# How batch 0 is fetched and normalised in the opening of a fused linear-attention and ELU-MLP kernel

## The chip, the cores and the metric

The kernel runs on one core of a Trainium2 chip. The metric is device time in microseconds (us) from launch to end. The kernel before took 285.53 us, the median of four runs that lie between 285.08 and 285.66 us. A separate execution was recorded by the hardware profiler; where the text speaks of the profile or the trace, it is that one execution.

## The reference, cut to what matters

```
kv  = einsum('bhsd,bhse->bhde', k, v)          # 8 batches, 8 heads, 576 positions, head size 64
out = einsum('bhsd,bhde->bhse', q, kv)
rms = sqrt(mean(out*out, axis=-1) + 1e-06)
att = out / rms * g_norm                       # per head
x   = att.transpose(0, 2, 1, 3).reshape(4608, 512)
h   = x @ w_in                                 # 512 -> 2048
g   = where(h > 0, h, exp(min(h, 0)) - 1)
y   = g @ w_out                                # 2048 -> 512
```

There is no softmax: each head has a 64 by 64 product K'V, which is multiplied by Q, normalised over the 64 features and scaled by a gain. The rest is a two-layer MLP. All inputs and the output are fp32; the kernel multiplies in bf16.

## The kernel before, in words

The 4608 rows of the MLP are worked in nine tiles of 512 rows. For each tile the kernel forms the normalised attention rows, turned so that features lie on partitions (`xT`), multiplies them by `w_in` (`mm1`, eight pairs of 128 columns, line 382), applies ELU (`elu`, lines 343 to 373) and multiplies by `w_out` (`mm2`, line 403). TensorE (PE) runs its instructions in the order in which the program issues them; there is no scheduler, since the whole program is recorded under a manual schedule, and each engine keeps program order.

Q, K and V of one batch are four chunks of 128 partitions by 576 numbers each; a chunk holds two heads. In fp32 a chunk is 288 KB, in bf16 144 KB. Tile 0 is mostly batch 0, and it is built chunk by chunk in a special opening (lines 577 to 652), which the change rewrites. For chunk c the steps are: `chunk_kv` (18 small matmuls, line 156), `chunk_kv_out` (VectorE (DVE) copies the product to SBUF, line 112), `chunk_y` (two matmuls of the turned Q with it, line 189), `chunk_square` (ScalarE (ACT), line 551), `mean_mm` (a matmul with a matrix of ones, line 199), a logarithm and an exponential on ACT for the inverse root (`inv_t` or `chunk_norm`), and `chunk_scale` (DVE, line 212), which writes row block c of `xT`. `early` (line 569) issues the first-layer matmuls of tile 0 for one row block c of `w_in` and `xT` at a time: pairs of columns (0,0) to (2,1), in the order c = 0, 2, 1, 3. `idle` (line 525) issues matmuls of zeros, as filling between waits.

Data comes on three issue queues. SyncE's queue (SP) brings chunks 0 and 2 of Q, and chunk 0 of K and of V, in fp32 into staging tiles, and `first_cast` turns them to bf16 on ACT and DVE. ACT's queue brings only the gain. GpSimd's queue (POOL) brings everything else and casts it to bf16 during the transfer: the other chunks of batch 0 (lines 488 to 494), then `w_in` in row blocks 0, 2, 1, 3 for the first six column blocks (line 496), the rest of `w_in`, then `w_out` alternating with batch 1, then batch 2. POOL's transfers take turns over eight semaphores, so the ninth is issued only when the first has landed, the tenth when the second has, and so on. Q is turned on PE with `ident` (`turned_q`, 16 transposes for two chunks, line 174) and copied out by DVE (`q_t_out`).

From batch 2 on Q arrives in fp32, is cast on POOL (`cast_q`, line 103), turned by a DMA transpose on SP's queue (`turn_q`, line 331), and only after that turn has landed does `after_turn` (line 339) let POOL issue the loads of the next batch. Attention rows of tiles from 2 on are also turned by DMA (`xT<-xs`, line 306) and then scaled by the gain (line 312).

## Time and profile before

| what | us |
|---|---|
| median of four runs | 285.53 |
| profiled execution, whole | 287.11 |
| its span, first to last instruction | 285.3 |
| PE busy in the span | 277.0 (97%) |
| DVE busy | 165.3 (58%) |
| ACT busy | 141.5 (50%) |
| POOL busy | 48.4 (17%) |
| granted TensorE clock | 0.999 of full |

The profile page gives busy time by engine, the span in 40 slices, the chain of work that ended last, and groups of like instructions. The timeline gives single groups of instructions in order of time: start, duration, engine, line, operation, and in brackets the idle time of the engine before it and what ended it. PE is matmul, PEld is the load of the stationary operand, which runs beside it. Matmuls are pipelined and their ends are modelled. The time from the issue of a transfer to its landing comes from the semaphore that tells of it.

### The profile page before, as it was taken

How to read it: one execution, taken by the hardware profiler on the slowest of the kernel's cores; microseconds unless marked ns; L12 is line 12 of the kernel's file. 1: busy time of each engine (PE TensorE's matmuls, PEld its weight loads, DVE VectorE, ACT ScalarE, POOL GpSimd, SP SyncE). 2: the span in 40 equal slices, each digit the busy share in tenths (PEclk: the TensorE clock that was granted, in tenths of full speed). 3: DMA queues.
4: the chain of work that ended last, by engine and by line, in shares of the span. 5: the costliest groups of instructions: out<-in, count | busy, mean ns of one | idle time of the engine just before them, and what ended most of it. 6: DMA issues, size and time to landing. Idle time of an engine off the chain costs nothing.

```text
span 285.3 us, 5154 instructions
## 1 busy us (share of the span) xinstructions
PE 277.0 (97%) x2123; PEld 128.9 (45%) x2123; DVE 165.3 (58%) x222; ACT 141.5 (50%) x209; POOL 48.4 (17%) x89
## 2 busy tenths in 40 slices
PE   7899999999799999999999999999999999999994
PEld 3434444443444444444444444444444444444443
DVE  3449532866487657854775378627763776344600
ACT  3778359694467355425552455345543554333311
POOL 7743303304340033032102220000000000000000
PEclk9999999999999999999999999999999999999999
DMA  7999999899996689779637971612150234020222
GB/s 210 191 204 206 207 263 224 199 283 128 183 292 83 142 168 251 99 181 256 159 36 159 261 166 40 150 45 74 39 110 0 74 39 110 0 76 0 74 74 75
DMA packets 50571, 39.46 MB, mean 138 GB/s; under 512 B 30964, under 2 KB 44020, under 8 KB 50548
## 3 DMA queue, kind: packets, MB, share of 16 engines
q0 software_dynamic: 15008, 21.30, 37.3%
q1 hardware_dynamic: 35136, 17.31, 29.3%
q10 hardware_dynamic: 404, 0.53, 0.5%
q8 instruction: 16, 0.26, 0.4%
q14 instruction: 7, 0.06, 0.1%
HBM read 36.70 MB, written 9.44 MB: 162 GB/s over the span
## 4 chain that ended last, share of the span: by engine, by line
PE 87%; DMA 6%; DVE 2%; ACT 2%; POOL 1%; issue 0%; SPq 0%; DVEq 0%; POOLq 0%
PE h_ps L382 40%; PE o_ps L403 39%; DMA xT<-xs 3%; DMA v_bf<-in_v_dram 2%; PE at L250 2%; PE at L156 1%; PE o_ps L440 1%; PE h_ps L569 1%; ACT elu_e L350 1%; DVE gT L366 1%; POOL k_bf L90 1%; PE mean L199 0%; PE qt_ps L174 0%; PE kv_ps L156 0%; PE y_ps L189 0%
## 5 line engine op out<-in xcount | busy, mean ns | idle before, releaser
L403 PE MATMUL o_ps<-w_out_sb,gT 128*128 128x512 bf16 x560 | 129.9, 379 | 0.0
L382 PE MATMUL h_ps<-xT,w_in_sb 128*128 128x512 bf16 (+1 forms) x560 | 128.0, 376 | 1.9 <-DVE xT L312 1.8
L350 ACT ACTIVATE elu_e<-h_ps 128x1024 bf16<-128x1024 f32 (+1 forms) x79 | 74.0, 953 | 91.3 <-PE h_ps L382 89.6
L403 PEld LDWEIGHTS <-gT 128*128 128x128 bf16 x560 | 54.3, 98 | 66.1 <-issue 0.9
L382 PEld LDWEIGHTS <-w_in_sb 128*128 128x128 bf16 x560 | 53.1, 98 | 63.3 <-issue 2.5
L366 DVE TENSOR_TENSOR gT<-elu_e,h_ps 128x1024 bf16<-128x1024 bf16 (+1 forms) x67 | 77.2, 1157 | 6.9 <-PE h_ps L382 0.5
L362 DVE TENSOR_SCALAR elu_e<-elu_e 128x1024 bf16<-128x1024 bf16 x72 | 31.9, 443 | 64.6 <-ACT elu_e L350 64.5
L419 ACT COPY o_sb<-o_ps 128x512 f32<-128x512 f32 x32 | 18.4, 588 | 21.2 <-PE o_ps L403 21.2
L103 POOL CAST q_bf<-st_q 128x384 bf16<-128x384 f32 x36 | 17.1, 519 | 42.1 <-DMA st_q<-in_q_dram 42.1
L283 DVE TENSOR_REDUCE ss<-sq 128x16 f32<-128x1024 bf16 x14 | 17.1, 1219 | 6.8 <-ACT sq L277 6.8
L299 DVE TENSOR_TENSOR xs<-at,ss 128x1024 bf16<-128x1024 f32 x14 | 17.1, 1219 | 1.9 <-ACT ss L292 1.9
L277 ACT ACTIVATE sq<-at 128x1024 bf16<-128x1024 f32 x14 | 14.4, 1028 | 0.0
L212 DVE SCALAR_TENSOR_TENSOR xT<-y_ps,g_col,rT 128x512 bf16<-128x512 f32 (+1 forms) x10 | 6.2, 640 | 10.1 <-ACT rT L209 8.0
L339 POOL COPY gate<-qT 1x16 bf16<-1x16 bf16 x5 | 1.1, 211 | 58.0 <-DMA qT<-q_bf 58.0
L355 ACT ACTIVATE elu_h<-h_ps 128x1024 bf16<-128x1024 f32 (+1 forms) x12 | 9.3, 821 | 0.0
L312 DVE TENSOR_SCALAR xT<-xT,g_col 128x1024 bf16<-128x1024 bf16 x14 | 6.7, 481 | 3.9 <-DMA xT<-xs 3.9
L156 PEld LDWEIGHTS <-k_bf 64*64 64x64 bf16 x576 | 6.4, 107 | 5.4 <-issue 5.4
L90 POOL DMA_DIRECT2D v_bf<-in_v_dram x11 | 7.8, 711 | 4.2 <-DMA w_in_sb<-in_moe_w_in_dram 2.1
L90 POOL DMA_DIRECT2D k_bf<-in_k_dram x11 | 7.7, 702 | 2.9 <-DMA w_in_sb<-in_moe_w_in_dram 2.2
L250 PEld LDWEIGHTS <-qT 64*128 64x128 bf16 (+1 forms) x248 | 4.3, 97 | 6.1 <-issue 5.9
L112 DVE COPY o_sb<-o_ps 128x256 f32<-128x256 f32 x1 | 0.4, 425 | 11.1 <-PE o_ps L440 11.1
L366 DVE TENSOR_TENSOR gT<-elu_e,elu_h 128x1024 bf16<-128x1024 bf16 x9 | 6.3, 704 | 0.8
(57 smaller groups left out, 101.4 us busy)
## 6 DMA issues: line engine op xcount, KB each, us to landing
st_q<-in_q_dram POOLq DMA_DIRECT2D x6, 1152.0 KB, 8.1
out_dram<-o_sb SPq DMA_DIRECT2D x24, 256.0 KB, 3.4
k_bf<-in_k_dram POOLq DMA_DIRECT2D x6, 576.0 KB, 10.4
v_bf<-in_v_dram POOLq DMA_DIRECT2D x6, 576.0 KB, 12.9
out_dram<-o_sb SPq DMA_DIRECT2D x19, 128.0 KB, 2.4
w_out_sb<-in_moe_w_out_dram POOLq DMA_DIRECT2D x4, 512.0 KB, 14.7
w_in_sb<-in_moe_w_in_dram POOLq DMA_DIRECT2D x2, 512.0 KB, 11.1
q_bf<-in_q_dram POOLq DMA_DIRECT2D x3, 288.0 KB, 13.4
```

The source lines that it names most:

```text
L90: eng.dma_start(out=dst.rearrange("p m j d -> p m (j d)"), in_=in_[:, ms, :])
L103: nc.gpsimd.tensor_copy(out=bf["q", b][:, u, js], in_=raw[b][:, u::2, js, :].rearrange("p l j d -> p j l d"),)
L250: nc.tensor.matmul(se_ps[lo:hi, l, (4 * i + m) * 64 : (4 * i + m) * 64 + 64], lhsT=qT[b][l * 64 : l * 64 + 64, s, u, j : j + n, :], rhs=kv ...
L277: nc.scalar.activation(sq, st["se", h], AF.Square)
L283: nc.vector.reduce_sum(out=ss, in_=st.pop(("sq", h)).rearrange("p l (m e) -> p (l m) e", e=D), axis=AX.X,)
L299: nc.vector.tensor_tensor(out=st["xs"][:, 2 * h : 2 * h + 2, :].rearrange("p i (l m e) -> p l i m e", l=2, e=D), in0=se_ps.rearrange("p l ...
L350: nc.scalar.activation(e[:, lo:hi, :], h, AF.Exp)
L362: nc.vector.tensor_scalar(out=e, in0=e, scalar1=1.0, scalar2=1.0, op0=ALU.min, op1=ALU.subtract)
L366: nc.vector.tensor_tensor(out=gT[T][:, 2 * i + lo : 2 * i + hi, :], in0=e[:, lo:hi, :], in1=h, op=ALU.add if relu else ALU.max,)
L382: nc.tensor.matmul((ps[a] if isinstance(ps, list) else ps[:, a, :])[:, cols], lhsT=w_in_sb[:, c, f * P : f * P + P], rhs=xT[T][:, c, cols] ...
L403: nc.tensor.matmul(o_ps[T, j], lhsT=gT[T][:, f, j * P : j * P + P], rhs=w_out_sb[:, f, :], start=(f == 0), stop=(f == FC - 1),)
L419: nc.scalar.copy(o_sb[T, half][:, j % 2, :], o_ps[T, j])
```

## The change: what it does

Six things are changed, all in the opening.

- On SP's queue now come chunk 0 of Q, then chunk 0 of V, then the gain; on ACT's queue comes chunk 0 of K. SP no longer brings chunk 2 of Q.
- Chunk 2 of Q is loaded on POOL's queue with a cast, ahead of everything else on that queue; it makes POOL's list of transfers one longer.
- The casts of chunk 0 are whole: Q on DVE, K and then V on ACT. DVE no longer casts a part of V, and ACT no longer casts a part of Q.
- Q of chunk 0 and of chunk 2 are turned apart, eight transposes and one 64-partition copy each (`turned_chunk`), instead of sixteen transposes and one 128-partition copy. Chunk 2 is turned after K'V of chunk 0.
- The product of chunk 0 with Q comes ahead of K'V of chunk 2. The logarithm of the first norm is issued before the square of chunk 2, and its exponential after it. The same is done with chunks 1 and 3: product and square of chunk 1 come ahead of K'V of chunk 3, and the mean and logarithm of chunk 1 ahead of the product and square of chunk 3 and of the first `early` group.
- The matmuls of zeros are 16 instead of 18, and the transpose of the gain comes after the first turn.

```diff
-    def first_load(name, cs):
+    def first_load(name, eng):
-        st = stage.tile([P, len(cs), RK, D], FP32, name=f"first_{name}", tag=f"first_{name}")
-        load(st, name, 0, slice(cs[0], cs[-1] + 1, 2), nc.sync)
+        st = stage.tile([P, 1, RK, D], FP32, name=f"first_{name}", tag=f"first_{name}")
+        load(st, name, 0, slice(0, 1), eng)
...
-    first = {"q": first_load("q", (0, 2)), "k": first_load("k", (0,)), "v": first_load("v", (0,))}
+    first = {}
+    for name, eng in (("q", nc.sync), ("k", nc.scalar), ("v", nc.sync)):
+        first[name] = first_load(name, eng)
...
-    nc.scalar.dma_start(out=g_row, in_=g_src)
+    nc.sync.dma_start(out=g_row, in_=g_src)
...
+    chunk_load("q", (2,))
     chunk_load("k", (2,))
     chunk_load("v", (2,))
...
+    def first_cast(name, eng):
+        copy_on(eng, bf[name, 0][:, 0:1], first[name])
+
+    def turned_chunk(l):
+
+        half = slice(l * 64, l * 64 + 64)
+        ps = as_bf16(single("m", "qt_ps"))
+        for j in range(8):
+            nc.tensor.transpose(ps[half, j * P : j * P + P], bf["q", 0][:, 2 * l, j, :], ident)
+        nc.vector.tensor_copy(
+            out=qT[0][half, :, 0, 0:8, :],
+            in_=ps[half].rearrange("p (j s r) -> p s j r", s=2, r=64),
+        )
...
-    idle(10, kv_ps[:, 0, :])
+    idle(9, kv_ps[:, 0, :])
+    first_cast("q", V)
+    first_cast("k", A)
+    turned_chunk(0)
     nc.tensor.transpose(g_ps[:, 0, 0:1], g_row.rearrange("o l e -> o (l e)"), one)
-    first_cast("q", (0, 2), V, low)
-    first_cast("q", (0, 2), A, high)
     nc.vector.tensor_copy(out=g_col, in_=g_ps[:, 0, 0:1])
-    ps = turned_q(0, 0, "m")
-    idle(3, kv_ps[:, 0, :])
-    first_cast("k", (0,), A, slice(0, RK))
-    q_t_out(0, 0, V, ps, slice(0, 8))
-    first_cast("v", (0,), A, high)
-    first_cast("v", (0,), V, low)
     mean = pair("A", "mean")[:, 0, :]
+    idle(2, kv_ps[:, 0, :])
+    first_cast("v", A)
     chunk_kv(kv_ps, 0)
     chunk_kv_out(kv_ps, 0, V)
+    turned_chunk(1)
+    chunk_y(0, single("x", "y_ps"))
+    chunk_square(0)
     chunk_kv(kv_ps, 2)
     chunk_kv_out(kv_ps, 2, V)
-    chunk_y(0, single("x", "y_ps"))
-    chunk_square(0)
-    idle(1, mean)
-    chunk_y(2, single("x", "y_ps"))
-    chunk_square(2)
     idle(1, mean)
     mean_mm(sq0[0], mean)
     r = r_tile()
-    inv_t(r[:, 0, :], mean)
-    mean = single("m", "mean")
+    nc.scalar.activation(r[:, 0, :], mean, AF.Ln, bias=eps_col)
+    chunk_y(2, single("x", "y_ps"))
+    chunk_square(2)
+    nc.scalar.activation(r[:, 0, :], r[:, 0, :], AF.Exp, scale=-0.5)
     ps = turned_q(0, 1, "m")
     q_t_out(0, 1, V, ps, slice(0, 8))
+    kv_ps = pair("B", "kv_ps")
+    h_ps = [pair("A", "h_ps")]
+    idle(1, h_ps[0][:, 0, :])
+    mean = single("m", "mean")
     mean_mm(sq0[2], mean)
     inv_t(r[:, 1, :], mean)
-    kv_ps = pair("B", "kv_ps")
-    h_ps = [pair("A", "h_ps")]
     chunk_kv(kv_ps, 1)
     chunk_kv_out(kv_ps, 1, V)
+    chunk_scale(0, r[:, 0, :])
     idle(2, h_ps[0][:, 0, :])
-    chunk_scale(0, r[:, 0, :])
+    chunk_y(1, single("m", "y_ps"))
+    chunk_square(1)
     chunk_kv(kv_ps, 3)
     chunk_kv_out(kv_ps, 3, V)
-    chunk_y(1, single("m", "y_ps"))
-    chunk_square(1)
     idle(1, h_ps[0][:, 0, :])
+    mean = single("m", "mean")
+    mean_mm(sq0[1], mean)
+    chunk_scale(2, r[:, 1, :])
+    r = r_tile()
+    nc.scalar.activation(r[:, 0, :], mean, AF.Ln, bias=eps_col)
     y3 = single("x", "y_ps")
     h_ps += [None, [single("x", "h_ps"), None]]
     chunk_y(3, y3)
     chunk_square(3)
-    chunk_scale(2, r[:, 1, :])
     h_ps[1] = pair("B", "h_ps")
     early([(0, 0), (0, 1)], 0)
-    mean = single("m", "mean")
-    mean_mm(sq0[1], mean)
-    r = r_tile()
-    nc.scalar.activation(r[:, 0, :], mean, AF.Ln, bias=eps_col)
     early([(1, 0), (1, 1), (2, 0)], 0)
```

## The prediction

> **What bounds the kernel now.** I read the page's busy shares, PE's waits, then the chain in order of time, then the timeline around each place where PE and a landing meet. The waits of PE come first:

> ```profile
> PE h_ps L382 <- DVE xT L312: 1.8, 1, 1.8
> PE kv_ps L525 <- DVE one L518: 1.2, 1, 1.2
> PE kv_ps L156 <- DVE v_bf L112: 0.5, 1, 0.5
> PE kv_ps L156 <- DVE kv_sb L112: 0.4, 1, 0.4
> PE kv_ps L156 <- DMA v_bf<-in_v_dram: 0.3, 1, 0.3
> PE h_ps L569 <- DVE xT L212: 0.2, 1, 0.2
> ```

> These 4.4 us are all of PE's larger waits: five before 16.4 us, one (1.8) at 71 us. A gain needs PE's useful work to slide forward, so I ask what holds it in place. The chain, in order of time (start, us, what):

> ```profile
> 4.95 7.02 DMA v_bf<-in_v_dram
> 11.97 0.14 issue
> 12.10 0.38 PE kv_ps L156 x13
> ...
> 14.22 0.70 ACT rT L632
> ...
> 16.32 2.17 PE h_ps L569 x9
> ...
> 62.56 9.64 DMA xT<-xs
> ```

> The opening's chain runs through V of chunk 3, which lands at 11.97, then K'V, mean, logarithm, scale, and at 16.32 the five first-layer matmuls with row block 1. The weight loads of PE say what comes 1.5 us later:

> ```profile
> 16.32 1.17 PEld L569 LDWEIGHTS <-w_in_sb 128*128 128x128 bf16 x6 [0.47 <-issue]
> 17.87 1.19 PEld L569 LDWEIGHTS <-w_in_sb 128*128 128x128 bf16 x7 [0.37 <-DMA w_in_sb<-in_moe_w_in_dram]
> ```

> After seven matmuls of 0.216 us (five with row block 1, two of pair (2,1)), so at 16.32 + 1.51 = 17.83, PE needs row block 3 of `w_in`. That transfer is issued at 9.34 and takes 8.49, so it lands at 17.83. PE and the transfers arrive together: an earlier PE only waits there. The same row of PEld shows another `w_in` wait at 21.07, and by issue and landing times `w_out`'s second block lands at 32.93 (needed 32.98) and its fourth at 42.37 (needed 42.6).

> The transfers themselves never rest. Windows of 4 us (us, PE, PEld, DVE, ACT, POOL busy, clock, DMA share, GB/s):

> ```profile
> 44.00:48.00 4.00, 4.00 (x20) 1.84 (x19) 1.50 (x2) 3.94 (x8) 2.17 (x5) 1.00 1.20 209
> 64.00:68.00 4.00, 4.00 (x21) 1.82 (x19) 3.28 (x4) 3.07 (x6) 2.96 (x6) 1.00 1.23 194
> 68.00:72.00 4.00, 3.08 (x14) 1.04 (x12) 1.46 (x3) 0.88 (x2) 0.00 (x0) 1.00 1.46 67
> ```

> From 3 us to 50.8 us the share is near or over 1: one queue of loads, in fixed order. At its end Q of batch 2 lands (45.78), is cast and turned (landed 52.42), and only that releases batch 3's loads at 52.99. These run to 71.74, and the turns of tile 2 beside them take 9.64 us against a median of 2.5, to 72.21. After 72.89 PE has no wait left: 212.4 us follow. So the end is 72.9 plus a constant, and 72.9 hangs on a line of transfers that began at 3 us.

> [...]while SP's and POOL's queues both ran (5.0 to 6.5 us) they read about 385 KB/us together by the packet records (a casting load reads twice what it writes), POOL's alone later 404. [...]The gain's four packets on ACT's queue, issued at 0.77 to 1.97, moved only at 4.0, as the 576 KB of Q ahead of them ended; [...]so K on ACT's queue should come right after Q. [...]SP's first packet came 0.6 us after its issue, POOL's only 2.4 after the end of its own; I use the trace.

> **The change, part by part** (against the profiled span, 285.3; the median of the runs, 285.53, lies 0.2 above it, and the whole profiled execution, 287.11, 1.8 above).

> *Transfers.* Before V of chunk 3 has landed, twelve chunks must come, before and after. One chunk takes 0.72 us either way: as fp32 on SP's queue at full rate (288 KB at 400 KB/us), as a cast on POOL's (landings of K1, V1, K3, V3 at 9.78, 10.51, 11.26, 11.97). After the change hardware queues carry three chunks instead of four and POOL's nine instead of eight. POOL's stream starts at 4.55, where before 764 of 1152 KB were over, leaving 388 KB (0.97 us) and 8 x 0.72: 6.73 us. After: 864 - 764 = 100 KB (0.25) and 9 x 0.72: 6.73. The same. Weighing 385 against 404 KB/us for the shorter time of sharing gives at most 0.1 us of gain. POOL's issue list grows by one of 0.56 us, so V3 is issued near 5.5 instead of 4.95, with 6 us to spare. The first `w_in` load now waits for Q of chunk 2 (I estimate 6.2; issue then about 6.2 instead of 5.47, its data due at 12); every later one waits for the same landing as before. So row block 3 lands at 17.7 to 17.85, and the line up to 72 stands.

> *First landings.* Q alone: its 288 KB (295 thousand bytes) are through at 3.35 by the rates of the one-us windows (25, 134, 392, 374 GB/s from 1 to 5 us), and 0.6 more to landing, as before: 3.95. K on ACT: through at 4.1, landed 4.7 (before 5.42). V: 5.5 (before 6.91). The gain, behind V on SP: 5.7; not hidden, since its transpose stands on PE ahead of K'V.

> *Casts and turn.* DVE casts Q 4.0 to 4.53 (0.58 for 640 wide, so 0.53). ACT casts K 0.67 to 5.42, V 0.67 from 5.55 to 6.22, where DVE and ACT shared V in 0.41. Nine idles of 0.413 end at 4.9, eight transposes at 5.36, copy 0.69 to 6.1; the gain's transpose at 5.75, two idles to 6.47. K'V of chunk 0 starts at 6.47 instead of 7.31: 0.84 earlier. The second half-copy is one more DVE instruction of 0.69, at 7.37 to 8.06; DVE idles there, and the product of chunk 2, which needs it, stands at 8.8. Two idles fewer: nothing, PE has waits there.

> *Norm chain on ACT.* The first square starts at 7.9 (before 8.85). From it: square 0.63, mean and handover 0.49, logarithm 0.69, square of chunk 2 0.63, exponential 0.63, logarithm 0.69, exponential 0.63: 12.28. Square of chunk 1 to 12.91 (its product is ready at 11.96, so ACT is the later one; before, PE was); mean 0.49; logarithm 0.69 to 14.09; square of chunk 3, 0.63, now ahead of the exponential; halves 0.36 each to 15.44; half-scale and handover 0.57: 16.01. Row block 1 starts at 16.06 instead of 16.32. Behind the waiting mean of chunk 1 stand, on PE, chunk 3's product (13.2) and the first `early` group; its `w_in` landed at 13.32 anyway, so about 0.1 is lost there and covered by a mean fewer further on.

> *Sum.* PE reaches row block 3 at 16.06 + 1.51 = 17.57 and waits 0.25 for 17.82. Gain on the path: 0.26 - 0.26 = 0, plus 0 to 0.1 from the transfers. Span 285.25; time 285.5.

> **Rivals.**
> 1. *The opening comes late (slower).* K and V are cast one after the other on ACT, and the gain lies behind V. If K lands at 5.9 or the gain at 6.5 (ACT's issue took 1.20 us before, beside a table load of 1.28), my sum puts K'V 0.8 later, ACT's chain follows one to one, and after the 0.25 of slack row block 3 starts 0.55 late. It decides from a K'V start past 6.7. At 7.7 it is 1.0 us: 286.5. Against it: the 1.8 us of idle at 71 should absorb it, if the turns land with batch 3's loads and not with their own issue.
> 2. *The transfers start faster.* From 2 to 3 us only 134 GB/s flowed, at 392 after. If two queues fill that hole by half, everything moves by 0.3; if the turns at 72 move more than the loads do, 0.7: 284.8. Against it: the engines were already 0.8 to 0.96 busy in that hole, with slow packets.
> 3. *Two queues don't do what they say:* K waits for V, because its issue completes later. Then K'V starts at 6.95, row block 3 at 18.05, 0.2 late: 285.7, which I count with no change.

> **How the numbers follow.** I give the tie, rival 3 with it, 0.70; rival 1 0.18; rival 2 0.12. About 0.2%, 0.57 us, is what a measurement of this kernel can tell from no change: faster 0.12 below 284.96, same 0.70, slower 0.18 above 286.1. Predicted 285.5. The range takes in 0.1 to 0.5 from the transfers and the runs' own spread of 0.3 below, and most of rival 1 above: 284.8 to 286.3.

> **What would show it.** Right: K'V of chunk 0 near 6.5, row block 1 near 16.1, then a wait of PEld for `w_in` ended near 17.8, landings from 9 us on unchanged within 0.2, a PE wait of about 1.8 us at 71. Wrong: row block 3 landing before 17.4 (the stream is not bound as I say), or matmuls of row block 1 after 16.4 (the ACT chain), or the wait at 71 grown or shrunk by more than 0.5.

## The result, and the profile after

| | before | after |
|---|---|---|
| median of the runs, us | 285.26 (63 runs, 284.83 to 287.06) | 285.92 (44 runs, 285.35 to 289.40) |
| profiled execution, us | 287.11 | 285.93 |
| its span, us | 285.3 | 284.2 |
| PE busy in the span, us | 277.0 | 277.5 |
| last matmul to the end of the span, us | 3.85 | 4.18 |

The changed kernel takes 1.0029 times the time before, with an interval of 1.0019 to 1.0039: 0.66 us more between the medians, where the prediction said no change. The 285.92 itself lies inside the range that was given, 284.8 to 286.3; but that range stood around the 285.53 of four runs, and the kernel before comes out at 285.26 in 63.

The two profiled executions can't simply be subtracted. The one of before, 287.11, lies above all of its 63 runs, and only ten of these are over 286. A second profiled execution of the same kernel (286.25) has a wait of 1.16 us at 71 us instead of 1.81. Two kernels that hardly differ from it have none: d3 below, which differs only in the weights that some early matmuls read (285.28), and e2 below, with one memset moved (285.49). In these two, the last load of batch 3 (its V) lands at 69.59 and 69.58, in the first profile of before at 71.74. So the wait at 71 us, on which the prediction leaned, goes with executions above the median; those near it seem not to have it.

PE's waits after the change (engine, line, what it waited for, then us in total, times, longest):

```profile
PE kv_ps L527 <- DVE eps_col L519: 1.2, 1, 1.2
PE h_ps L582 <- DMA w_in_sb<-in_moe_w_in_dram: 0.7, 1, 0.7
PE kv_ps L156 <- DMA v_bf<-in_v_dram: 0.4, 1, 0.4
```

The two waits for DVE in the opening (`v_bf` and `kv_sb`, 0.9 us together) are gone, and so is the wait at 71 us. The windows of 4 us there (columns as in the prediction) show PE without a gap:

```profile
64.00:68.00 4.00, 4.00 (x20) 1.84 (x19) 3.10 (x5) 3.60 (x7) 2.40 (x5) 1.00 1.25 196
68.00:72.00 4.00, 4.00 (x23) 2.06 (x22) 2.61 (x5) 0.52 (x2) 0.00 (x0) 1.00 0.94 122
```

In their place stands one new wait of 0.7 us, for `w_in`. The chain, in order of time, leads into it:

```profile
2.12 5.25 DMA k_bf<-in_k_dram
7.37 0.28 issue
7.65 0.53 POOL w_in_sb L116
8.18 0.16 issue
8.34 8.63 DMA w_in_sb<-in_moe_w_in_dram
16.97 0.05 issue
17.02 2.13 PE h_ps L582 x9
```

Before, this chain ran through V of chunk 3, ACT's logarithm and DVE's scale into the same matmuls at 16.32. Now it is a transfer: row block 1 of `w_in` lands at 16.97, where it landed at 15.25 before. PE's timeline says how early PE was (start, duration, engine, line, operation, and in brackets the wait before it):

```profile
15.54 0.81 PE L582 MATMUL h_ps<-xT,w_in_sb 128*128 128x512 bf16 x3
17.02 3.19 PE L582 MATMUL h_ps<-xT,w_in_sb 128*128 128x512 bf16 x14 [0.66 <-DMA w_in_sb<-in_moe_w_in_dram]
```

The end of a PE group is modelled; the last of these three matmuls starts at 15.97, and they follow each other by 0.22. DVE's scale of chunk 1 ended at 15.96. So without this landing the five matmuls would have begun at about 16.2, 0.8 earlier (in d1 below, where they don't wait for it, the same two starts are 15.89 and 16.10). Row block 3 then follows at 18.54, 0.67 later than before, with no wait of its own (it had landed at 17.36).

The second new thing is at the very end. The last matmul's result is copied by DVE and stored. First before, then after:

```profile
280.67 0.82 PE L440 MATMUL o_ps<-w_out_sb,gT 128*128 128x256 bf16 x6
281.58 0.42 DVE L112 COPY o_sb<-o_ps 128x256 f32<-128x256 f32 x1 [11.10 <-PE o_ps L440]
```

```profile
279.27 0.71 PE L440 MATMUL o_ps<-w_out_sb,gT 128*128 128x256 bf16 x5
280.42 0.42 DVE L112 COPY o_sb<-o_ps 128x256 f32<-128x256 f32 x1 [11.45 <-DMA out_dram<-o_sb]
```

The matmuls end at 281.49 and 279.98. The copy starts 0.09 us after them before, and 0.44 after the change. The instruction and the semaphores it waits for are the same in both programs, and so is everything behind it.

### The profile page after: what moved, and what is told of

It is laid out like the page before. It is cut to its first block, busy times and chain, and to the rows that moved or that the text cites. A ratio compares the mean times of both kernels' runs of the same rounds, so it can differ in the third digit from the quotient of the medians.

```text
span 284.2 us, 5146 instructions
## 1 busy us (share of the span) xinstructions
PE 277.5 (98%) x2121; PEld 129.5 (46%) x2121; DVE 165.5 (58%) x222; ACT 140.9 (50%) x208; POOL 49.5 (17%) x90
## 4 chain that ended last, share of the span: by engine, by line
PE 91%; DMA 6%; DVE 1%; POOL 1%; ACT 0%; issue 0%; POOLq 0%; DVEq 0%
PE o_ps L403 43%; PE h_ps L382 42%; DMA w_in_sb<-in_moe_w_in_dram 3%; DMA k_bf<-in_k_dram 2%; PE at L250 2%; PE at L156 1%; PE h_ps L582 1%; DMA out_dram<-o_sb 1%; PE o_ps L440 1%; PE qt_ps L174 0%; DVE gT L366 0%; PE mean L199 0%; ACT elu_e L350 0%; PE kv_ps L156 0%; PE y_ps L189 0%
## 5 line engine op out<-in xcount | busy, mean ns | idle before, releaser
L382 PE MATMUL h_ps<-xT,w_in_sb 128*128 128x512 bf16 (+1 forms) x560 | 128.0, 376 | 0.1
L382 PEld LDWEIGHTS <-w_in_sb 128*128 128x128 bf16 x560 | 53.2, 98 | 61.3 <-issue 0.5
L103 POOL CAST q_bf<-st_q 128x384 bf16<-128x384 f32 x36 | 17.9, 539 | 39.1 <-DMA st_q<-in_q_dram 39.1
L212 DVE SCALAR_TENSOR_TENSOR xT<-y_ps,g_col,rT 128x512 bf16<-128x512 f32 (+1 forms) x10 | 6.2, 640 | 10.0 <-ACT rT L209 7.9
L156 PEld LDWEIGHTS <-k_bf 64*64 64x64 bf16 x576 | 6.4, 107 | 5.0 <-issue 4.2
L312 DVE TENSOR_SCALAR xT<-xT,g_col 128x1024 bf16<-128x1024 bf16 x14 | 6.7, 481 | 1.8 <-DMA xT<-xs 1.8
L112 DVE COPY o_sb<-o_ps 128x256 f32<-128x256 f32 x1 | 0.4, 424 | 11.5 <-DMA out_dram<-o_sb 11.5
```

The costliest lines, as they stand in the source:

```text
L103: nc.gpsimd.tensor_copy(out=bf["q", b][:, u, js], in_=raw[b][:, u::2, js, :].rearrange("p l j d -> p j l d"),)
L382: nc.tensor.matmul((ps[a] if isinstance(ps, list) else ps[:, a, :])[:, cols], lhsT=w_in_sb[:, c, f * P : f * P + P], rhs=xT[T][:, c, cols] ...
```

## The experiments

Each was timed in turn with the kernel before on the same chip; the ratio is to that kernel, with its interval. "Landing" is the last of the 16 steps that a transfer has in the semaphore events of the trace: for row block 1 after the change the first is at 14.95, the 15th at 15.99 and the 16th at 16.97, and PE starts behind the 16th, at 17.02. I read each step as one of the 16 DMA engines being done, so that an engine that is late shows as a distance between the 15th and the 16th.

### The same two kernels again

> The changed kernel as it is, for a second trace. My theory (fetch): the 16 KB read of TensorE's own instructions, which the trace shows at 14.95 us in the changed kernel and at 15.75 us in the kernel before, holds one of the 16 DMA engines for about 1 us; in the changed kernel it hits row block 1 of w_in (15 engines done by 16.0, the last at 16.97), in the kernel before it hits row block 3 (15 done by 16.2, the last at 17.82), and only the first of these stands in PE's way. It expects 0.6 to 0.9 us slower than before, and in this trace again the matmuls of row block 1 behind that block's last engine, or, if the read falls elsewhere in this execution, a span that follows. Rival (late stream): the changed kernel is late because V of chunk 3 lands 0.42 us later (12.39 against 11.97), whatever the read hits. It expects the same time, and row block 1's matmuls to start late even where the block's last engine is early.

> The kernel before, for a second trace: its first trace is of an execution of 287.11 us, 1.9 us above its median, and holds a wait of TensorE of 1.8 us at 71 us. I expect an execution near 285.0 to have a smaller wait there or none, the read of instructions near 15.7 us again, no slow packets between 5 and 9 us, and the matmuls of row block 1 between 16.0 and 16.4.

After: 286.17, ratio 1.0036 (1.0021 to 1.0051), 22 runs from 285.31 to 287.96. The slowdown is there again in a series of its own. Its profiled execution (286.93) waits in other places: row block 1 isn't late (matmuls at 16.30), but row block 3 lands at 18.12, and there are waits of 0.40 at 21.58, 0.29 at 33.58, 0.16 at 42.19 and 0.35 at 71.85. The second profiled execution of before (286.25) has row blocks 1 and 3 at 16.32 and 17.82, as the first. So the place of the wait moves between executions, and no single one of them can carry the whole of the loss.

The start of the work moves too. K'V of chunk 0 begins at 7.15 in this second execution of the changed kernel, at 6.67 in the first. The clock of PE is recorded as full from 6.85 us on here, from 5.76 there; over all twenty profiles of this text that moment lies between 3.95 and 7.19. Ahead of it a matmul of zeros takes 0.43 us, behind it 0.22. Of the kernels with the new loads, a1, b2, c2 and c4 (and b1, which waits longer for V) have the full clock only from 6.76 us or later, and in these four K'V begins at 7.10 to 7.33. Little of a1's delay is left where row block 1 starts: 16.30, against the 16.2 worked out above.

### Fewer matmuls of zeros

The changed kernel has two fewer. What they are worth, by leaving out seven of the 16 (first), the same with one of the other nine replaced by eight short ones (second), and eight of the 18 in the kernel before (third). The lines that the first leaves out:

```
-    idle(2, kv_ps[:, 0, :])
-    idle(1, mean)
-    idle(1, h_ps[0][:, 0, :])
-    idle(2, h_ps[0][:, 0, :])
-    idle(1, h_ps[0][:, 0, :])
```

> The changed kernel without seven of its idle matmuls (all but the first nine): 14 rows fewer in TensorE's program ahead of the first-layer matmuls, nothing else. Fetch theory: [...]the read comes at 16 us or later and hits row block 3 or what follows; row block 1 lands near 15.3 and PE gains 0.6 to 0.7 us: about equal to the kernel before (ratio 0.999 to 1.001). Late stream: V of chunk 3 lands as late as in the changed kernel, the time stays 0.7 to 0.9 us above before (ratio 1.003).

> The same without the seven idles, but one of the first nine idles (512 columns) is replaced by eight idles of 64 columns, so the number of rows in TensorE's program is again that of the changed kernel, at about the same time. Fetch theory: the read is back near 15 us and on row block 1, slower than before by 0.6 to 0.9 us (ratio 1.002 to 1.003). Late stream, or a theory in which the idles themselves cost: as the kernel without the seven idles, within 0.2 us.

> The kernel before without eight of its idle matmuls (all but the first ten), 16 rows fewer. Fetch theory: the read moves from 15.75 to after 17 us, row block 3 then lands near 16.2 instead of 17.8; PE reaches it at 17.83 either way, so no change (ratio 0.999 to 1.001), at most 0.2 us gained. A theory in which the idles keep TensorE fast: slower by some tenths.

All three are slower: 287.08, ratio 1.0055 (1.0034 to 1.0076); 286.97, 1.0064 (1.0041 to 1.0086); 287.47, 1.0075 (1.0052 to 1.0098). For the last, two windows of 4 us:

```profile
8.00:12.00 4.00, 3.58 (x49) 1.79 (x43) 0.61 (x3) 2.20 (x4) 2.80 (x5) 0.50 1.21 205
12.00:16.00 4.00, 3.39 (x43) 1.59 (x44) 2.65 (x5) 2.83 (x5) 3.14 (x5) 0.50 1.12 184
```

The third number from the end is the granted clock: half speed, from 7.36 to 17.60 us in all, where the kernel before has full speed from 4.87 us, its first record of the clock, past its last matmul. Row block 1 starts at 19.14 there. This stretch at half speed is 10.24 us long, three times 3.41; the one in the second kernel, 13.35 to 16.76, is 3.41. In the 3.41 us ahead of the fall in the third kernel PE was busy for 1.74. Two of the three profiles with fewer zeros have a fall, and none of the four of the kernel before and the changed kernel has one (mean clock 0.997 to 0.999). The profile of the first kernel has no fall, but the mean clock that its runs were granted is 0.984 to 0.994 in eight of twelve; the other four, at 0.996 or more, took 285.50 to 286.86, as the changed kernel does. The changed kernel itself keeps enough zeros: in its two profiles the clock, once full, stays so past the last matmul, and only one of its 44 runs (289.40) was granted as little as 0.994. So the two zeros it lost are not the cause.

### The loads or the order

The new order with the old loads, and the new loads with the old order:

```
# b4: new order, old loads
-    for name, eng in (("q", nc.sync), ("k", nc.scalar), ("v", nc.sync)):
-        first[name] = first_load(name, eng)
+    first = {"q": first_load("q", (0, 2)), "k": first_load("k", (0,)), "v": first_load("v", (0,))}
...
-    chunk_load("q", (2,))
```

```
# c4: new loads and casts, old order of product, mean and logarithm
-    chunk_y(0, single("x", "y_ps"))
-    chunk_square(0)
     chunk_kv(kv_ps, 2)
     chunk_kv_out(kv_ps, 2, V)
+    chunk_y(0, single("x", "y_ps"))
+    chunk_square(0)
...
```

> The changed order of the work with the loads of the kernel before: Q of chunks 0 and 2 in fp32 on SP with K and V of chunk 0, the gain on ACT, nothing new on POOL; chunk 2 of Q is cast on ACT ahead of K. Late stream theory: no slow packets, V of chunk 3 at 11.97, and the time within 0.3 us of before. Fetch theory alone: the rows are those of the changed kernel, so the read should fall near 15 us and row block 1 be late here too: 0.5 to 0.9 us slower. If the new order of the norms costs by itself: slower too, but with the scale of chunk 1 done after 16.3.

> The changed loads, casts and turns with the old order of products, squares, means and scales from K'V of chunk 0 on. The converse kernel (new order, old loads) took 286.2 and was 0.55% slower with no slow packet. If the loss of the changed kernel comes with the loads (last engine of 16 late), this one is slower than before by 0.5 to 1.0 us as well. If it comes with the order of the norms, this one equals the kernel before within 0.2 us or is faster.

The new order alone: 286.21, ratio 1.0055 (1.0036 to 1.0073). V of chunk 0 lands at 7.25, K'V starts at 7.99, and row block 1 at 17.05. Five of its 16 runs had a fall of the clock (0.992 or less, 287.39 and more); the median of the others is 286.12. The new order needs the new loads. The new loads and casts with the old order: 285.49, ratio 1.0011 (0.9999 to 1.0023), some 0.3 us, which the interval doesn't separate from nothing. Its waits show the same landing:

```profile
PE y_ps L189 <- DVE kv_sb L112: 0.6, 2, 0.4
PE h_ps L582 <- DMA w_in_sb<-in_moe_w_in_dram: 0.5, 1, 0.5
PE kv_ps L156 <- DMA v_bf<-in_v_dram: 0.3, 1, 0.3
```

So perhaps 0.3 us goes with the loads, and the order adds about as much again although PE's opening is no later with it. That second part shows at the end of the kernel (below).

### Slow packets

In the packet records, POOL's queue has no packet over 0.18 us between 4.6 and 9 us in the kernel before, nor in any run with the old loads; every run with the new loads has 2 to 26 of them, against a median of 0.107; up to 0.77 us in the changed kernel. At the landing of V of chunk 3, four of the 16 engines of the changed kernel are 0.5 to 0.7 us behind the middle one, and V lands at 12.39 instead of 11.97. In a2, with only two slow packets, it lands at 11.87. Three attempts to find what makes them: all hardware loads on one queue (b1), Q of chunk 2 behind K and V of chunk 2 on POOL's queue (c2), and one more load that nobody reads, to keep SP's queue busy as long as before (c3).

```
# b1
-    for name, eng in (("q", nc.sync), ("k", nc.scalar), ("v", nc.sync)):
+    for name, eng in (("q", nc.sync), ("k", nc.sync), ("v", nc.sync)):
# c2
-    chunk_load("q", (2,))
     chunk_load("k", (2,))
     chunk_load("v", (2,))
+    chunk_load("q", (2,))
# c3
+    extra = stage.tile([P, 1, RK, D], FP32, name="extra", tag="extra")
+    load(extra, "v", 0, slice(2, 3), nc.sync)
```

> The changed kernel with chunk 0 of K again on SP's queue and the gain on ACT's: one hardware queue, all else as changed. In three of four traces with the changed loads, POOL's stream meets packets of 0.2 to 0.9 us between 5.2 and 7.1 us (12, 16 and 26 of over 0.18 us; the kernel before has none), three to five of the 16 DMA engines fall 0.5 to 0.7 us behind, and V of chunk 3 lands near 12.4 instead of 11.97. If two queues at once cause this, this kernel has none, V of chunk 3 lands near 12.0 and the time falls to within 0.3 us of before. If it comes from POOL's queue carrying Q of chunk 2 and running alone from 5.2 us, the slow packets and the late landing stay: 0.6 to 0.9 us slower than before.

> The changed kernel with chunk 2 of Q loaded behind chunk 2 of K and V on POOL's queue, and turned after K'V of chunk 2: the same transfers, another order. If Q of chunk 2 in first place disturbs POOL's stream, the slow packets go, V of chunk 3 lands near 12.0 and the time falls to within 0.4 us of before. If the stream is disturbed because it runs alone from 5.2 us, they stay and the time is that of the changed kernel, 0.6 to 1.0 above before.

> The changed kernel with one more load, which nothing reads: chunk 2 of V in fp32 on SP's queue behind the gain, so that the hardware queues are busy until 6.5 us as before. Thirteen chunks now come instead of twelve, so V of chunk 3 should land at 12.7 or later, and the time should be 0.7 us or more above before for that alone. What tells the theories apart is the packets: with the stream alone early as the cause, fewer than four of over 0.18 us between 4.6 and 9 us; with the loads' order as the cause, ten or more as in the changed kernel.

None removes them: 15, 9 and 18 slow packets. The times are 289.43 (1.0136, 1.0102 to 1.017), 285.80 (1.0032, 1.0018 to 1.0046) and 286.65 (1.0045, 1.0032 to 1.0058). In b1 one packet of POOL's queue took 1.68 us; Q and K of chunk 0 landed earlier than with two queues (3.69 and 4.31), but V at 9.51, and PE stood for its cast:

```profile
PE kv_ps L156 <- ACT v_bf L110: 3.1, 1, 3.1
```

After that wait the clock of b1 was at half from 10.33 to 13.74 us. Five of its six runs were granted 0.992 or less and took 289.25 or more; the sixth, at 0.998, took 286.74. So most of b1's loss is V's late landing and the fall of the clock after it, and the run doesn't say what the second queue is worth without them. The profile of c3 has a fall as well (11.18 to 14.60), and four of its 22 runs. What makes the packets slow stays open; only the tie to the changed loads is seen.

### TensorE's own instructions

Row block 1 landed at 16.97, but 15 of its 16 engines were done at 15.99. The packet records hold something that lasts about that long: packets of 16,384 bytes on an instruction queue (q8 on the page), 16 in the run, 0.9 to 1.5 us each, the first about 0.95. I take them for reads of TensorE's instructions, since with 42 records more on PE (b3 below) there are 17 of them and the first comes at 12.75, and I take each to hold one engine. The first is read at 14.95 after the change and at 15.75 before. In twelve executions (us: read time, then how far the last engine lies behind the 15th on row blocks 1 and 3):

```
kernel                        read    block 1   block 3
before                        15.75    0.06      1.61
before, again                 15.54    0.08      1.66
before, fewer zeros (a4)      15.20    0.00      1.28
new order, old loads (b4)     15.39    0.12      1.42
Q of chunk 2 later (c2)       15.22    0.01      1.10
after, again (a1)             15.96    0.25      0.91
after                         14.95    0.98      0.42
old order, new loads (c4)     14.74    1.38      1.13
after, fewer zeros (a2)       14.49    1.32      0.90
the same with short ones (a3) 14.87    1.62      1.35
before, more rows (b3)        12.75    0.89      0.91
after, fewer rows (b2)        15.11    0.23      0.95
```

In these, a read before 15.0 goes with a late row block 1, which PE needs at 16.3; with a later read, row block 3 is the late one, which PE needs only at 17.8. It isn't strict: of the six executions that came after, three don't fit (d2: read at 14.79, row block 1 only 0.30 behind; e3: 15.19, 1.94 behind; e2: 15.83, and neither row block more than 0.03 behind). Nor did the read move as expected with fewer zeros: in a2 and a4 it should have come after 16 and 17 us, and came at 14.49 and 15.20, earlier than in the kernels they were made from. To move it on purpose, I changed how many instructions stand on PE: wider matmuls of zeros in fp32 in the changed kernel, meant to be 21 fewer, and 42 more in the kernel before (24 narrow ones for three wide).

```
# b2
-    idle(9, kv_ps[:, 0, :])
+    idle(1, kv_ps[:, 0, :])
+    idle2(4, kv_ps[:, 0, :])
# b3
-    idle(10, kv_ps[:, 0, :])
+    idle(7, kv_ps[:, 0, :])
+    pad(24, kv_ps[:, 0, :])
```

> The changed kernel with pairs of idle matmuls replaced by one fp32 idle matmul of about the same time, so TensorE's program has 21 rows fewer ahead of the first-layer matmuls and its clock should not fall, as it did where idles were left out (half speed for 3.4 and 10 us in two of those). Fetch theory: the 16 KB read of instructions moves from 15 to 16.5 us or later; row block 1's last engine is then at most 0.3 us behind the fifteenth, the matmuls of row block 1 start at 16.3 to 16.5 instead of 17.0, and the time falls by 0.3 to 0.7 us. Late stream alone: the time stays 0.6 to 0.9 above before.

> The kernel before with three of its first ten idle matmuls replaced by 24 idle matmuls of 64 columns, which take about the same time: 42 rows more in TensorE's program, nothing else. Fetch theory: the read moves about 1 us earlier, to 14 to 15 us, and holds row block 1 (or block 2); row block 1 lands near 16.5 instead of 15.25, its matmuls start there, and the kernel is slower by 0.3 to 1.0 us (ratio 1.001 to 1.0035). Late stream: no change, within 0.2 us, with V of chunk 3 at 11.97.

In b3 the read moves by far, and the late engine with it (the last row but one). In b2 the edit did not do what it was meant to: in the trace each fp32 matmul of zeros is two weight loads and two matmuls, so the zeros are 32 records of PE, as in the changed kernel, and the read at 15.11 is within what that kernel shows by itself. And the time doesn't judge: b2 is 285.89 (1.0029, 1.0019 to 1.0039), and in its profile the full clock came only at 7.06 and K'V at 7.33; b3 is 286.03 (1.0027, 1.0015 to 1.0039), with row block 1 started 0.2 late, at 16.54, by an opening that was late (full clock at 6.78, K'V at 7.85) and not by its landing at 15.93. Both are inconclusive. The read isn't set by the program alone: the same kernel read at 14.95 and at 15.96.

### The wait for row block 1 taken away

So the wait itself was removed. In the early matmuls, row block 1 of `xT` (d1), or row blocks 1 and 3 (d2, and d3 in the kernel before), read the weights of row block 2, which have landed long before; that part of the first layer is computed with wrong weights.

```
-                lhsT=w_in_sb[:, c, (2 * i + a) * P : (2 * i + a) * P + P],
+                lhsT=w_in_sb[:, {1: 2}.get(c, c), (2 * i + a) * P : (2 * i + a) * P + P],
```

> The changed kernel, but the five early matmuls of tile 0 with row block 1 of `xT` read the weights of row block 2, which have landed already (that part of the first layer is computed with wrong weights). Nothing else moves; only the wait for the landing of row block 1 is gone. Theory A (the loss is the wait for the last engine of row block 1): these matmuls start at about 16.4 instead of 17.0, those of row block 3 near 17.9, and the time falls by 0.3 to 0.7, to 285.2 to 285.5. Theory B (the transfers or the opening are late as a whole, and row block 1 is only where it is seen first): PE waits for row block 3 or a later block of `w_in` instead, and the time stays at 285.8 to 286.1.

> The same with row blocks 1 and 3 of `w_in` both read as row block 2 in the early matmuls (again wrong weights in that part). Theory A: as the run without the wait for row block 1, or 0.1 to 0.3 less, 285.0 to 285.5. Theory B, transfers late: 0.5 or more below the run that leaves out row block 1 alone. Theory B, opening late: both stay at 285.8 to 286.1.

> The same two row blocks read as row block 2 in the kernel before (wrong weights in that part). If row block 3 bound the start of tile 0 as the prediction says, with PE arriving at the same time, the time is within 0.2 of the kernel before, 285.1 to 285.3. If the landings of `w_in` cost the kernel before something in most executions, it falls by 0.3 or more, and then theory A has to be judged by the difference between the two kernels without these waits.

d1: 285.72, ratio 1.0021 (0.9997 to 1.0045). d2: 285.68, 1.0020 (1.0006 to 1.0035). d3: 285.27, 1.0005 (0.9992 to 1.0018). Theory A falls in its size: the medians put the wait at about 0.2 us (285.92 to 285.72), not 0.3 to 0.7, and the intervals of the two ratios overlap. In d1, PE starts row block 3 at 17.76, about as early as in the kernel before, and still the time is 0.5 longer. It doesn't start earlier because DVE's scale of chunk 3 ends only at 17.71:

```profile
16.83 0.88 DVE L212 SCALAR_TENSOR_TENSOR xT<-y_ps,g_col,rT 128x256 bf16<-128x256 f32 x2 [0.95 <-ACT rT L575]
17.76 0.31 PEld L582 LDWEIGHTS <-w_in_sb 128*128 128x128 bf16 x2 [0.26 <-issue]
```

The same scale ends at 17.60 in the kernel before, so the new order brings this one no earlier. A part of what PE won is given back at the next landing. PE's timeline of d1:

```profile
32.11 0.75 PE L174 MATMUL qt_ps<-ident,q_bf 128*64 128x128 bf16 x20
33.14 1.02 PE L403 MATMUL o_ps<-w_out_sb,gT 128*128 128x512 bf16 x4 [0.29 <-DMA w_out_sb<-in_moe_w_out_dram]
```

This is the second block of `w_out`. The prediction had named it as due at 32.93 and needed at 32.98. In d1 it lands at 33.10. Over all executions with the old loads it lands at 32.69 to 33.13, median 32.93 (seven, e2 below among them), with the new ones at 32.84 to 33.83, median 33.21 (eleven, b1 and c3 left out): 0.28 later, the size of c4's loss. And from the last matmul on, d1 takes 4.18 us, d2 4.21 and d3 3.85. That is most of what lies between d2 and d3, the two kernels that wait for neither row block: 285.68 and 285.27 (0.41 apart, with intervals that overlap).

### The last copy

That 0.33 us is the same in all 17 profiled executions but e1 to e3 below: 3.83 to 3.85 us from the last matmul to the end in every kernel with the old order, 4.13 to 4.21 in every one with the new order, whatever its loads. The records of DVE's sequencer (semaphore waits count as instructions; number from the start, start and end in us, first before, then after) show why the copy is late:

```
317 268.432 268.482 wait              316 267.790 267.840 wait
318 276.971 277.021 wait              317 276.325 276.375 wait
319 277.421 280.670 wait for PE       318 276.423 280.028 wait for PE
320 280.713 281.138 copy              319 280.423 280.847 copy
```

(The left column is the second profiled execution of before.) Usually one record follows the end of a wait after 0.045 us. Before, 0.40 us pass between records 318 and 319; after, 0.395 between the same two numbers. The same stop comes 128 records earlier in both: 0.40 us behind record 190 (after the change, behind its start). Another 128 records earlier, behind record 62, there is none (after the change the next record starts 0.012 us after it), so a stop doesn't come after every 128 records. The packet records have a mark of each stop, in all twenty profiles: a packet of 8,192 bytes on an instruction queue, which begins 1.2 to 1.5 us after record 191 and 0.65 to 0.93 us after record 319, at 278.09 in the left column and at 281.10 in the right. As the packet begins after the stop is over, it can't be for this packet's data that the engine stands.

The new order needs one separate semaphore wait fewer on DVE ahead of `chunk_scale`, so DVE has 324 records instead of 325, everything after it moves up by one, and the stop that lay ahead of the wait for the last matmul, hidden by it, now lies behind it. The two stops seen lie 128 records apart and add 0.35 us each to the usual 0.045; with a wait behind it, as before, the last stop leaves the copy 0.09 us after the matmul, without one 0.44. What the sequencer does in them is not shown.

Three runs on it: one DVE instruction more in the changed kernel, one fewer in the kernel before, and the first together with d2's edit.

```
# e1, e3
     turned_chunk(1)
+    nc.vector.memset(spare, 0.0)
# e2
-    nc.vector.memset(one, 1.0)
+    nc.gpsimd.memset(one, 1.0)      # ahead of make_identity
```

> The changed kernel with one more DVE instruction in the opening, a fill of one column (0.06 us, in idle time of DVE, read by nothing). Theory C: DVE's sequencer stops for 0.35 us after every 128 instructions; in the changed kernel, which has one DVE instruction fewer than the kernel before, the third such stop falls between the wait for the last matmul and the last copy of the output, so it is on the path. With one instruction more it falls ahead of that wait again: the last copy starts 0.09 us after the last matmul instead of 0.44, and the time falls by 0.35, to 285.5 to 285.6. Theory D (the 0.35 at the end belongs to the changed loads, or is given back elsewhere): the last copy starts at 0.44 still, or the time stays at 285.8 to 286.1.

> The kernel before with one DVE instruction fewer: the constant `one` is filled on POOL, which costs POOL some 0.05 us ahead of its loads. Theory C: the last copy starts 0.44 us after the last matmul instead of 0.09, and the time rises by 0.35 to 0.4, to 285.5 to 285.65. Theory D: it stays at 285.1 to 285.3.

> The changed kernel with the one DVE instruction more, and row blocks 1 and 3 of `w_in` read as row block 2 in the early matmuls (wrong weights in that part). If the stop of DVE at the end (0.35) and the waits for these row blocks are the whole loss, the time is that of the kernel before with the same edit, 285.2 to 285.4. If the late transfers or the order of the opening cost something besides, it stays at 285.5 or more.

e2: 285.53 against 285.09, ratio 1.0022 (1.0008 to 1.0035). One DVE instruction fewer costs the kernel before 0.44 us (0.2 to 1.0 by the interval). The memset now stands on POOL ahead of its loads, but the loss isn't there: the last matmul of its profile ends at 279.51, no later than d3's at 279.63. Its copy:

```profile
278.81 0.71 PE L440 MATMUL o_ps<-w_out_sb,gT 128*128 128x256 bf16 x5
279.96 0.42 DVE L112 COPY o_sb<-o_ps 128x256 f32<-128x256 f32 x1 [11.45 <-DMA out_dram<-o_sb]
```

It starts 0.44 after the last matmul, where before has 0.09, and the name in the bracket is that of the changed kernel too. (The view puts the idle down to a store of the output, for which the waits ahead of the copy had already been passed; the stop itself has no name there.)

e1's copy does move back to 0.09, but its time doesn't follow: 286.08, ratio 1.0031 (1.002 to 1.0043), six runs, one at 285.23 and five from 285.96 to 286.29. e3 likewise: 286.29 (1.0045, 1.0031 to 1.0059), six runs. Three of PE's waits in e1, with its 1.2 at the start and 0.6 for the gain left out:

```profile
PE h_ps L382 <- DVE xT L312: 0.5, 1, 0.5
PE h_ps L382 <- DVE gT L366: 0.3, 1, 0.3
PE o_ps L403 <- DMA w_out_sb<-in_moe_w_out_dram: 0.3, 1, 0.3
```

These waits are of the kind that a1 has too (0.3 for `xT`, 0.4 for `gT`, 0.3 for `w_out`), so by themselves they don't tell e1 from the changed kernel. The second block of `w_out` lands at 33.43 in e1 and 33.53 in e3, with 15 engines done at 31.98 and 32.03; one engine is 1.5 us behind, more than in any other run. A slow-packet delay of 0.5 to 0.7 and an instruction read of 0.95 on the same engine would add up to that, which is only argued. Whether the extra DVE instruction has any part in it, or these six runs each met late transfers for other reasons, stays open; the changed kernel itself was not run beside them. That the stop costs the changed kernel 0.35 us is so seen in the records of DVE, and not confirmed by a time.

## Why the prediction was wrong

Rightly seen:

- *The first landings and K'V.* Q, K, V at 4.29, 4.50, 5.19 (predicted 3.95, 4.7, 5.5). That K would come right after Q was wrong: it came beside it. Between 2.0 and 4.0 us the packet records have 135 packets of SP's queue and 135 of ACT's, so the two queues moved side by side, in equal parts; Q landed 0.34 later than predicted and K 0.2 earlier. The eight transposes took 0.91 us, since the full clock came only at 5.76 (the other eight, behind it, took 0.63; the prediction had 0.46). So the gain's transpose ran at 5.98, and K'V starts at 6.67 instead of 6.47 (before 7.31).
- *The norm chain on ACT.* First square at 8.08 (7.9), square of chunk 1 at 12.52 (12.28), the scale of chunk 1 done at 15.96 (16.01). Without the transfer row block 1 would have started at about 16.2 (16.06). For chunk 1 the order of the opening costs and gains about what was worked out, 0.1 to 0.2 late. For chunk 3 nothing was worked out: its scale holds row block 3 until 17.76 in d1, where the prediction has PE there at 17.57.
- *PE and the transfers arrive together.* Removing PE's wait for one landing only brings it to the next thing it waits for (in d1 the scale of chunk 3, then the second block of `w_out`).

In the first profile all three signs of being wrong came: row block 3 landed at 17.36, row block 1 started at 17.02, and the wait at 71 was gone. The steps that failed:

- *"The same", for the stream of twelve chunks (step Transfers).* The count of bytes was right (POOL's first packet is at 4.65, not 4.55, which moves both sums alike), the rate wasn't: slow packets go with V of chunk 3 at 12.39, outside the 0.2 granted. This comes with the new loads, which with the old order cost some 0.3 us (c4, interval from nothing to 0.65), in line with the 0.28 at the second block of `w_out`.
- *"So row block 3 lands at 17.7 to 17.85" as the landing that counts.* Row block 3 landed at 17.36, earlier. Row block 1, which I had not priced since before it was over a microsecond ahead of need, landed at 16.97, one engine being 0.98 behind the others. By the medians it is worth about 0.2 us of the loss (d1), part of the 0.3 of the loads.
- *"So the end is 72.9 plus a constant" (What bounds the kernel now).* There are two errors in it. The wait of 1.8 us at 71 belongs to executions above the median (d3 and e2 have none), and where it is absent it can't absorb a delay of the opening. And what follows the last matmul, part of the constant, grew by 0.33 us, at the last copy, through a semaphore wait on DVE that the new order doesn't need. I counted DVE's instructions by their duration only.

Rival 1 named the right sign, but its mechanism isn't what cost the time. K landed at 4.50, and K'V started at 6.67 in the first profile, at 7.15, past the 6.7 at which this rival was to decide, in the second; there row block 1 still started at 16.30, as before. Rival 2 is refuted: from K of chunk 2 to 51 us every transfer but row block 3 arrived later than before. Rival 3 is refuted too, as K didn't wait for V.

The sum: 0.35 us for the stop before the last copy and about 0.3 for the loads would make the 0.66 between the medians. That the stop costs time is shown by e2, in the kernel before (0.44); the share of the loads rests on c4's uncertain 0.3 and on landings that are 0.28 later. That e1 didn't give the 0.35 back keeps this sum from being closed by a run, so how the 0.66 divides stays open. No kernel tried was faster than the kernel before.

## What to carry to other kernels

Before a profile's wait is counted as slack, ask whether the usual execution has it: compare the profiled time with the median. When a change lies at one end of a kernel, compare the other end too, from the last matmul on, since a shift of one instruction can lay bare a stop that was hidden (in e2 the last copy starts 0.44 us after its matmul, in before 0.09). Row block 1 landed with its slowest engine (16.97, the other 15 at 15.99), so a landing with little lead (15.25 for matmuls at 16.32 before) can become the bound though neither its bytes nor its place in the queue changed.
